# PSUM copies moved to ScalarE and spread over all banks outside the attention loops of a four-layer transformer kernel

## The chip, the cores and the metric

The kernel runs on one core of one Trainium2 chip. The metric is the device time of one launch in microseconds. TensorE (PE) multiplies matrices and transposes, VectorE (DVE), ScalarE (ACT) and GpSimd (POOL) work on elements, SyncE (SP) issues the DMAs.

## The reference

The input is one sequence of 2048 tokens of 512 bf16 features. Four residual layers A, B, A, B are applied, each to a layernorm of its input; both A layers share their weights, and so do both B layers.

```
A: q = x@wq (32 heads of 16); k = x@wk, v = x@wv (one head of 16, shared by all)
   o = softmax(q k^T / 4) v ;                       x += concat(o) @ wo
B: q,k,v = x@wqkv (32 heads of 16); phi(t) = where(t>0, t+1, exp(t)) + 1e-6
   o = phi(q) (phi(k)^T v) / (phi(q) . sum phi(k) + 1e-6) ;  x += concat(o) @ wo2
```

## The kernel before

Tokens lie in 16 tiles of 128 rows; x stays in SBUF (`x_sb`) from the first load to the last store. PSUM is one tensor of 8 banks (`ps_all`, `bank(i)`).

The order of the work is planned when the program is built. `add(engine, tau, ...)` gives each instruction a planned time tau, and each engine's instructions are issued in the order of tau. The tau only sort: the chip waits on semaphores, and each engine's queue is strictly in order. `plan(tau, task)` defers a part of the planning to its turn. A `Chain` is one PSUM bank with the event that last read it; a new user of the bank waits for that event.

The stages in order of time are:

1. **First prologue** (`a_prologue`). One DMA brings all of x, six more bring the weights, all counted on one semaphore, so that the first user of a weight (`ev_w`) waits for the last of them. Per tile, `ln_tile` computes layernorm (L305 statistics, L306 and L307 small steps on DVE, L309 a power on POOL, L314 the normalised tile into one of two `xn_buf` slots), PE transposes it (L322), DVE copies it to `xnT` (L325); `proj_session` (PE at L336) gives V, copied at L360. After every fourth tile, `block_task` gives four blocks of queries (L373) and the replicated keys (L379). Only banks 6 and 7 (`chain6`, `chain7`) are used, and DVE does every copy out of PSUM.
2. **Attention loop** (`a_loop`): 683 groups, in each three score matmuls into three banks (L449; banks 0 to 2 and 3 to 5 in turn), one exponential over them on ACT (L459) and twelve small matmuls with V (L478). After 8 units of a row tile its epilogue runs in bank 7: transposes (L517), copy (L522), output product (L534), residual add to x (L537). `on_x` then plans layer B's preparation of that tile (`b_prep_tile`): layernorm, key, value and, every fourth tile, four query projections, one after the other through bank 7. `phi_session` is one projection with phi: min(x,0) (L560) and max(x,0)+1e-6 (L561) on DVE, exp on ACT (L565), sum on DVE (L566). For tiles 0 to 14 this lies inside the loop, for tile 15 behind it.
3. **Layer B** (`b_main`): 64 matmuls gather phi(k)^T v (L619), four masked copies (L627), then per tile numerator and denominator (L646), two reciprocals (L661) and two products (L663), transpose (L675), copy (L685, DVE), output product (L693), residual add (L697). It uses banks 0 to 5.
4. The second layer A's prologue is planned tile by tile into the first `b_main`, behind each tile's residual add. Then the second loop and the second `b_main` follow, and 16 DMAs store x.

Of the kernel before, what the change touches and what calls it, by code (L numbers as in the profile page):

```python
# [150 lines left out]
def bass_interleave_layers__grouped_kv_mqa__linear_attn_block__prompt_kernel(  # L151
# [36 lines left out]
    xn_buf = sb("xn_buf", [P, 2, D], BF16)  # L188
# [76 lines left out]
    ev_x.tau = 8.0
    add(SP, 0.01, lambda e: e.dma_start(wk_sb[:], A_wk.rearrange("(ft f) c -> f ft c", f=P)), s_wdma, 16)
    add(SP, 0.02, lambda e: e.dma_start(wv_sb[:], A_wv.rearrange("(ft f) c -> f ft c", f=P)), s_wdma, 16)
    add(SP, 0.03, lambda e: e.dma_start(wq_sb[:], A_wq.rearrange("(ft f) c -> f ft c", f=P)), s_wdma, 16)
# [34 lines left out]
    def ln_tile(t, x_ev, tau, chain):
# [21 lines left out]
        evc = add(DV, evt.tau + 0.7 + HOP, lambda e, t=t, tpv=tpv: e.tensor_copy(xnT[:, :, t * P:(t + 1) * P], tpv), dv_a, waits=[evt])  # L325
# [3 lines left out]
    def proj_session(chain, tau, mml, ncols, w_mm, readers):  # L329
# [10 lines left out]
        for (eng, dtau, fn, sem_, xw) in readers:  # L340
            tr = _tmax(tr + dtau, [evm] + list(xw))
            evr = add(eng, tr, (lambda e, fn=fn, dst=dst: fn(e, dst)), sem_, waits=[evm] + list(xw))
            evs.append(evr)
# [451 lines left out]
```

## Time and profile before

| | us |
|---|---|
| median of 4 runs | 2143.38 (2143.09 to 2143.96) |
| the profiled execution | 2143.65 |
| its span, first to last instruction | 2141.8 |
| ACT busy in the span | 1880.0 (88%) |
| PE busy | 1737.6 (81%) |
| DVE busy | 571.3 (27%) |

The 1.85 us between the span and the time of that execution lie outside its instructions. The share of a busy engine is an average over stages: in the loops ACT is full, outside them it is nearly idle.

### The profile page before, as it was taken

The page shows a single profiled execution, that of the slowest core. Times are in us where ns is not written, and L with a number is a line of the kernel's source. Part 1 is how long each engine was busy: PE and PEld are TensorE (multiplying, and loading weights), DVE is VectorE, ACT ScalarE, POOL GpSimd, SP SyncE. Part 2 cuts the span into 40 slices and gives each one's busy share as a digit, 9 for nine tenths or more (in the row PEclk, how much of TensorE's full clock was granted, in tenths as well). Part 3 has the DMA queues.
Part 4 walks back from the last instruction along what each step waited for, and adds up shares of the span by engine and source line. Part 5 has one row for each costly group of instructions (what it writes and reads, how often), then busy time and mean ns, then how long its engine had stood idle before and what let it go on. Part 6 is the DMA issues. An engine that isn't in the chain of part 4 may idle for free.

```text
span 2141.8 us, 49091 instructions
## 1 busy us (share of the span) xinstructions
PE 1737.6 (81%) x22176; PEld 1011.1 (47%) x22176; DVE 571.3 (27%) x1648; ACT 1880.0 (88%) x1431; POOL 42.1 (2%) x80
## 2 busy tenths in 40 slices
PE   4888888888888888887678888888888888888876
PEld 2454454545455454444234544544544454444533
DVE  5221222112322222111680222322213121321227
ACT  0799999999999999998009999999999999999960
POOL 2000000000000000000010000000000000000000
PEclk9999999999999999999799999999999999999988
DMA  3000000000000000000000000000000000000001
GB/s 99 1 1 2 2 2 2 2 2 1 2 2 2 2 2 2 1 2 2 1 1 2 2 1 2 2 2 1 2 2 1 2 2 2 1 2 2 1 1 40
DMA packets 7746, 10.52 MB, mean 5 GB/s; under 512 B 1392, under 2 KB 7024, under 8 KB 7536
## 3 DMA queue, kind: packets, MB, share of 16 engines
q1 hardware_dynamic: 7536, 7.37, 1.1%
q8 instruction: 174, 2.85, 0.6%
q14 instruction: 36, 0.29, 0.0%
HBM read 5.28 MB, written 2.10 MB: 3 GB/s over the span
## 4 chain that ended last, share of the span: by engine, by line
ACT 43%; PE 36%; issue 11%; DVE 9%; DMA 0%; SPq 0%; POOL 0%; ACTq 0%; POOLq 0%
ACT PT L459 42%; PE ps_all L449 20%; PE ps_all L478 8%; PE ps_all L336 5%; PE ps_all L534 1%; ACT e_buf L565 1%; DVE Osb L663 1%; DVE Osb L501 1%; DVE x_sb L697 1%; DVE rdenA L495 1%; DVE stats L305 1%; DVE QT_sb L373 1%; PE ps_all L619 1%; DVE rdenB L661 1%; DVE xnT L325 0%
## 5 line engine op out<-in xcount | busy, mean ns | idle before, releaser
L459 ACT ACTIVATE PT<-ps_all 128x1536 bf16<-128x1536 f32 (+1 forms) x1366 | 1851.6, 1492 | 165.3 <-PE ps_all L449 163.4
L449 PE MATMUL ps_all<-qbd,Krep_sb 128*128 128x512 bf16 x4096 | 1115.1, 381 | 215.2 <-ACT PT L459 215.0
L478 PEld LDWEIGHTS ps_all<-Vaug,PT 128*128 128x128 bf16 x16384 | 619.4, 96 | 433.3 <-DVE Osb L501 110.8
L478 PE MATMUL ps_all<-Vaug,PT 128*128 128x17 bf16 x16384 | 640.2, 171 | 92.9 <-DVE Osb L501 91.1
L449 PEld LDWEIGHTS ps_all<-qbd,Krep_sb 128*128 128x128 bf16 x4096 | 301.0, 97 | 488.6 <-ACT PT L459 269.0
L495 DVE RECIPROCAL rdenA<-ps_all 128x4 f32<-128x4 f32 x256 | 46.7, 182 | 1152.2 <-PE ps_all L478 1152.2
L432 DVE TENSOR_TENSOR qbd<-QT_sb,mask 128x512 bf16<-128x512 bf16 x256 | 102.3, 416 | 0.0
L565 ACT ACTIVATE e_buf<-m_buf 128x512 f32<-128x512 f32 x64 | 41.3, 645 | 47.3 <-DVE m_buf L560 47.3
L309 POOL TENSOR_TENSOR rstd<-veps,mhalf 128x1 f32<-128x1 f32 x64 | 35.1, 548 | 2024.1 <-DVE veps L307 2014.5
L336 PE MATMUL ps_all<-wqkv_sb,xnT 128*128 128x512 bf16 x256 | 69.0, 393 | 3.8 <-DVE r_buf L561 2.8
L560 DVE TENSOR_SCALAR m_buf<-ps_all 128x512 f32<-128x512 f32 x64 | 44.2, 690 | 82.4 <-PE ps_all L336 82.4
L501 DVE TENSOR_TENSOR Osb<-ps_all,rdenA 128x64 bf16<-128x64 f32 x256 | 57.4, 224 | 8.9
L566 DVE TENSOR_TENSOR pk_tok<-e_buf,r_buf 128x512 bf16<-128x512 f32 x32 | 22.1, 692 | 104.2 <-ACT e_buf L565 104.2
L336 PE MATMUL ps_all<-xnT,wqkv_sb 128*128 128x512 bf16 x128 | 39.8, 441 | 11.0 <-DVE r_buf L561 9.2
L305 DVE BATCH_NORM_STATS2 stats<-x_sb 128x6 f32<-128x512 bf16 x64 | 44.1, 689 | 10.9 <-DMA x_sb<-in_A_x_dram 9.8
L336 PE MATMUL ps_all<-xnT,wq_sb 128*128 128x512 bf16 x128 | 40.9, 463 | 7.2 <-DVE QT_sb L373 3.8
L322 PE MATMUL ps_all<-ident,xn_buf 128*128 128x128 bf16 x256 | 27.2, 234 | 22.4 <-DVE xn_buf L314 19.4
L561 DVE TENSOR_SCALAR r_buf<-ps_all 128x512 f32<-128x512 f32 x64 | 43.6, 680 | 0.0
L693 PE MATMUL ps_all<-wo_sb,OT_sb 128*128 128x512 bf16 x128 | 33.1, 381 | 9.2 <-DVE OT_sb L685 9.2
L534 PE MATMUL ps_all<-wo_sb,OT_sb 128*128 128x512 bf16 x128 | 34.2, 390 | 1.0 <-DVE OT_sb L522 1.0
L537 DVE TENSOR_TENSOR x_sb<-x_sb,ps_all 128x512 bf16<-128x512 bf16 x32 | 22.0, 688 | 47.0 <-PE ps_all L534 47.0
L325 DVE COPY xnT<-ps_all 128x512 bf16<-128x512 bf16 x64 | 26.1, 408 | 24.3 <-PE ps_all L322 24.3
(46 smaller groups left out, 415.9 us busy)
## 6 DMA issues: line engine op xcount, KB each, us to landing
x_sb<-in_A_x_dram SPq DMA_DIRECT2D x1, 2048.0 KB, 8.9
out_dram<-x_sb SPq DMA_DIRECT2D x16, 128.0 KB, 1.7
wqkv_sb<-in_B_wqkv_dram SPq DMA_DIRECT2D x1, 1536.0 KB, 8.9
wq_sb<-in_A_wq_dram SPq DMA_DIRECT2D x1, 512.0 KB, 6.4
wo_sb<-in_A_wo_dram SPq DMA_DIRECT2D x1, 512.0 KB, 6.4
wo_sb<-in_B_wo_dram SPq DMA_DIRECT2D x1, 512.0 KB, 9.2
wk_sb<-in_A_wk_dram SPq DMA_DIRECT2D x1, 16.0 KB, 8.4
wv_sb<-in_A_wv_dram SPq DMA_DIRECT2D x1, 16.0 KB, 6.5
```

Source lines behind the costliest of these rows:

```text
L305: ev1 = add(DV, tau, lambda e, t=t: e.bn_stats(stats[:, t, 0:6], x_sb[:, t, :]), dv_a, waits=[x_ev])
L336: evm = add(PE, tp + k * EPS, (lambda e, l=l, r=r, k=k, n=n, dst=dst: e.matmul(dst, lhsT=l, rhs=r, start=(k == 0), stop=(k == n - 1))), pe ...
L432: qbd_ready[u] = add(DV, tq, (lambda e, u=u, qt=qt, g=g, half=half: e.tensor_tensor(out=qbd[:, u % NQBD, :].rearrange("p (a b) -> p a b", ...
L449: ev = add(PE, tsi, (lambda e, dst=dst, t=t, u=u: e.matmul(dst, lhsT=Krep_sb[:, t * P:(t + 1) * P], rhs=qbd[:, u % NQBD, :], start=True, s ...
L459: e_done[j] = add(AC, _tmax(tau_E(j), w), (lambda e, j=j, ng=ng, b0=b0: e.activation(PT[:, j % NPT, 0:ng * 512], bank(b0, ng * 512), ACTF. ...
L478: ev = add(PE, tpv, (lambda e, col0=col0, j=j, idx=idx, hh=hh, t=t: e.matmul(ps_all[:, col0:col0 + 17], lhsT=PT[:, j % NPT, idx * 512 + hh ...
L495: evr = add(DV, tn, (lambda e, accv=accv: e.reciprocal(rdenA[:, :].unsqueeze(2), accv[:, :, DH:DH + 1])), dv_a, waits=[ev_acc])
L501: acc_free[u] = add(DV, _tmax(tn + EPS / 4, wn, d=EPS / 8), (lambda e, qt=qt, quad=quad, accv=accv: e.tensor_tensor(out=Osb[:, qt % 2, qua ...
L534: evy = add(PE, t2 + g * EPS, (lambda e, g=g, qt=qt: e.matmul(bank(7), lhsT=OT_sb[:, qt % 2, g, :], rhs=wo_sb[:, g, :], start=(g == 0), st ...
L560: (DV, 0.0, (lambda e, src, s=s: e.tensor_scalar(out=m_buf[:, s, :], in0=src, scalar1=0.0, scalar2=None, op0=ALU.min)), dv_a, w_m),
L561: (DV, D_EVQ, (lambda e, src, s=s: e.tensor_scalar(out=r_buf[:, s, :], in0=src, scalar1=0.0, scalar2=1e-6, op0=ALU.max, op1=ALU.add)), dv_ ...
L565: ev_e = add(AC, _tmax(ev_m.tau + act_slack, w_e), (lambda e, s=s: e.activation(e_buf[:, s, :], m_buf[:, s, :], ACTF.Exp)), ac_a, waits=w_e)
```

## The change

1. x arrives in four DMAs of four tiles. The first is issued first, then wk, wv and wq on a semaphore of their own (`ev_wA`), then the rest of x and the other weights.
2. Each bank has a chain. `pick_chain` takes the one whose last planned use is oldest, among those that the loops or `b_main` don't hold at that planned time; in both it leaves what it left before (7 in the loop, 6 and 7 in `b_main`).
3. `copy_op` puts a copy on ACT when its planned time lies outside the loops (`act_free`), else on DVE. This holds for `xnT`, V, queries, keys, layer B's values and `OT_sb` of `b_main`.
4. Outside the loops phi's positive part is a Relu on ACT, then the min on DVE, the exp on ACT, and one DVE instruction adds e + 1e-6 + r.
5. Tile 15's preparation for layer B is planned with its six projections side by side in six banks (`parallel=True`). The gathering matmuls of `b_main` no longer wait for phi(q); each fourth tile of `b_main` waits for its block's phi(q).
6. Twelve matmuls whose result is read by nobody (`warm`) stand around the last epilogue of each loop: 2 ahead of the transposes, 2 behind them, 8 behind the output product.
7. `xn_buf` has three slots. Prologue tiles are planned 1.35 apart (1.7 before), block sessions 1.05 (0.6 before).

```diff
+    def act_free(tau):
+        return not _in(act_busy, tau, 2.0, 0.0)
+    def bank_ok(b, tau):
+        if b <= 5:
+            return not _in(s_busy, tau, 4.0, 1.0) and not _in(bmain_busy, tau, 1.0, 1.0)
+        if b == 6:
+            return not _in(act_busy, tau, 4.0, 2.0)
+        return True
+    def copy_op(tau, out_ap_fn, waits, prefer_act=True):
+        if prefer_act and act_free(tau):
+            return add(AC, tau, lambda e: out_ap_fn(e, True), ac_a, waits=waits)
+        return add(DV, tau, lambda e: out_ap_fn(e, False), dv_a, waits=waits)
...
-    ev_x = add(SP, 0.0, lambda e: e.dma_start(x_sb[:], xv), s_xdma, 16)
+    for c in range(4):
+        evd = add(SP, 0.001 * c, lambda e, c=c: e.dma_start(x_sb[:, 4 * c:4 * c + 4, :], xv[:, 4 * c:4 * c + 4, :]), s_xdmas[c], 16)
+        evd.tau = 2.5 * (c + 1)
+    add(SP, 0.0002, lambda e: e.dma_start(wk_sb[:], A_wk.rearrange("(ft f) c -> f ft c", f=P)), s_wA, 16)
+    add(SP, 0.0003, lambda e: e.dma_start(wv_sb[:], A_wv.rearrange("(ft f) c -> f ft c", f=P)), s_wA, 16)
+    ev_wA = add(SP, 0.0004, lambda e: e.dma_start(wq_sb[:], A_wq.rearrange("(ft f) c -> f ft c", f=P)), s_wA, 16)
...
+        L_end = tau_E(NGR) + 0.5
+        act_busy.append((L0, L_end))
+        s_busy.append((L0 - 2.5, L_end))
...
+        def warm(tau, n):
+            for k in range(n):
+                add(PE, tau + k * EPS / 8, (lambda e: e.matmul(bank(5), lhsT=Krep_sb[:, 0:P], rhs=QT_sb[:, 0, 0:512], start=True, stop=True)), None)
...
     def phi_session(chain, tau, mml, dst_ap, w_mm, act_slack):
+        if act_free(tau):
+            evs = proj_session(chain, tau, mml, 512, w_mm, [
+                (AC, 0.0, (lambda e, src, s=s: e.activation(r_buf[:, s, :], src, ACTF.Relu)), ac_a, w_m),
+                (DV, 0.6, (lambda e, src, s=s: e.tensor_scalar(out=m_buf[:, s, :], in0=src, scalar1=0.0, scalar2=None, op0=ALU.min)), dv_a, w_m),
+            ], serial=True)
...
+            ev_fin = add(DV, _tmax(ev_e.tau + 0.7 + HOP, [ev_e, ev_r]), (lambda e, s=s, dst_ap=dst_ap: e.scalar_tensor_tensor(
+                out=dst_ap, in0=e_buf[:, s, :], scalar=1e-6, in1=r_buf[:, s, :], op0=ALU.add, op1=ALU.add)), dv_a, waits=[ev_e, ev_r])
...
+            def ptask2():
+                RB["pk"][t] = phi_session(pick_chain(base), base, mml, pk_tok[:, t, :], [ev_xnT, ev_w], act_slack)
+                base += 4 * EPS
+                mml = [(xnT[:, ft, t * P:(t + 1) * P], wqkv_sb[:, ft, 2 * D:3 * D]) for ft in range(FT)]
+                evs = proj_session(pick_chain(base), base, mml, 512, [ev_xnT, ev_w], [
+                    ("copy", 0.0, mk_copy(lambda src, t=t: (vaugB_v[:, t, :, 0:DH], src.rearrange("p (h d) -> p h d", d=DH))), None, [ev_onesB])])
...
+                    for g in range(NG8):
+                        mml = [(wqkv_sb[:, ft, g * P:(g + 1) * P], xnT[:, ft, b * 512:(b + 1) * 512]) for ft in range(FT)]
+                        RB["pq"][(g, b)] = phi_session(pick_chain(base), base, mml, pqT[:, g, b * 512:(b + 1) * 512], xw, act_slack)
+                        base += 4 * EPS
...
-        w_all = list(RB["pk"]) + list(RB["v"]) + list(RB["pq"].values())
+        w_all = list(RB["pk"]) + list(RB["v"]) + [chains[b].last for b in range(6)]
...
-            evc = add(DV, _tmax(evt.tau + 0.7 + HOP, wc), (lambda e, t=t, tpv=tpv: e.tensor_copy(OT_sb[:, t % 2, :, :], tpv)), dv_a, waits=wc)
+            evc = copy_op(_tmax(evt.tau + 0.7 + HOP, wc), (lambda e, is_act, t=t, tpv=tpv: (e.copy if is_act else e.tensor_copy)(OT_sb[:, t % 2, :, :], tpv)), wc)
...
                 def on_x(qt, evx, RB=RB):
+                    if evx.tau > L_end - 12.0:
+                        b_prep_tile(qt, evx, RB, act_slack=0.3, gap=0.2, parallel=True)
+                    elif evx.tau > L_end - 40.0:
+                        b_prep_tile(qt, evx, RB, act_slack=0.3, gap=0.2)
+                    else:
+                        b_prep_tile(qt, evx, RB, act_slack=8.0, gap=1.0)
```

## Rows read from the trace of the kernel before

**Rows 1.** Busy time per engine in the stages, cut at the stage boundaries.
```profile
core 0: us, PE busy (x) PEld busy (x) DVE busy (x) ACT busy (x) POOL busy (x), PEclk, DMA share, GB/s
0.00:69.30 69.30, 38.25 (x213) 17.01 (x214) 39.37 (x118) 1.31 (x2) 15.79 (x32) 0.90 0.24 77
69.30:1012.80 943.50, 788.90 (x10585) 468.73 (x10583) 200.19 (x583) 936.16 (x710) 8.22 (x15) 1.00 0.01 2
1012.80:1048.20 35.40, 19.64 (x100) 8.87 (x100) 14.44 (x29) 3.15 (x5) 0.55 (x1) 0.57 0.00 0
1048.20:1123.60 75.40, 55.30 (x404) 26.45 (x405) 68.65 (x214) 0.00 (x0) 8.77 (x16) 0.98 0.00 1
```

**Rows 2.** Timeline of the first prologue: start us, us, engine, line, operation.
```profile
5.02 1.47 SPq L268 DMA_DIRECT2D wq_sb<-in_A_wq_dram  x1
...
9.77 0.69 DVE L305 BATCH_NORM_STATS2 stats<-x_sb 128x6 f32<-128x512 bf16 x1 [9.77 <-DMA x_sb<-in_A_x_dram]
...
12.74 0.41 DVE L325 COPY xnT<-ps_all 128x512 bf16<-128x512 bf16 x1
...
18.36 0.76 POOL L296 COPY wk_rep<-wk_sb 128x128 bf16<-128x128 bf16 x3 [5.50 <-DMA wo_sb<-in_B_wo_dram]
...
25.39 1.89 PE L336 MATMUL ps_all<-xnT,wq_sb 128*128 128x512 bf16 x4 [0.41 <-DVE Vaug L360]
...
63.04 1.04 PE L336 MATMUL ps_all<-xnT,wk_rep 128*128 128x512 bf16 x4 [0.70 <-DVE QT_sb L373]
...
69.27 8.16 ACT L459 ACTIVATE PT<-ps_all 128x1536 bf16<-128x1536 f32 x6 [67.18 <-PE ps_all L449]
```

**Rows 3.** Groups of ACT by shape: count, busy us, mean ns.
```profile
L459 ACT ACTIVATE PT<-ps_all 128x1536 bf16<-128x1536 f32 x1364 | 1849.7, 1493 | 165.3 <-PE ps_all L449 163.4
L565 ACT ACTIVATE e_buf<-m_buf 128x512 f32<-128x512 f32 x64 | 41.3, 645 | 47.3 <-DVE m_buf L560 47.3
L459 ACT ACTIVATE PT<-ps_all 128x1024 bf16<-128x1024 f32 x2 | 2.1, 1056 | 0.0
L459 ACT ACT_TABLE_LOAD x1 | 1.3, 1283 | 0.8 <-PEq L780 0.8
```

**Rows 4.** Groups of DVE by shape, from 1042 to 1126 us.
```profile
L373 DVE CAST QT_sb<-ps_all 128x512 bf16<-128x512 f32 x16 | 10.9, 680 | 3.0 <-PE ps_all L336 3.0
...
L685 DVE COPY OT_sb<-ps_all 128x512 bf16<-128x512 bf16 x16 | 6.6, 410 | 0.5 <-PE ps_all L675 0.5
...
L325 DVE COPY xnT<-ps_all 128x512 bf16<-128x512 bf16 x16 | 6.0, 378 | 0.2 <-PE ps_all L322 0.2
```

**Rows 5.** Timeline behind the first loop, tile 15's epilogue to `b_main`.
```profile
1016.17 0.69 DVE L537 TENSOR_TENSOR x_sb<-x_sb,ps_all 128x512 bf16<-128x512 bf16 x1 [1.98 <-PE ps_all L534]
...
1020.26 1.89 PE L336 MATMUL ps_all<-wqkv_sb,xnT 128*128 128x512 bf16 x4 [0.52 <-DVE xnT L325]
...
1041.79 5.42 PE L619 MATMUL ps_all<-vaugB,pk_tok 128*128 128x136 bf16 x64 [3.88 <-DVE pqT L566]
```

**Rows 6.** Timeline of the first `b_main` with the second prologue in it.
```profile
1048.22 0.41 PE L646 MATMUL ps_all<-kvzbd,pqT 128*128 128x136 bf16 x4 [1.01 <-DVE kvzbd L627]
...
1058.34 0.68 DVE L697 TENSOR_TENSOR x_sb<-x_sb,ps_all 128x512 bf16<-128x512 bf16 x1
...
1061.72 0.68 DVE L697 TENSOR_TENSOR x_sb<-x_sb,ps_all 128x512 bf16<-128x512 bf16 x1
...
1110.11 0.69 DVE L697 TENSOR_TENSOR x_sb<-x_sb,ps_all 128x512 bf16<-128x512 bf16 x1
...
1116.78 5.29 PE L336 MATMUL ps_all<-xnT,wq_sb 128*128 128x512 bf16 x16 [0.27 <-DVE Vaug L360]
...
1123.62 4.14 ACT L459 ACTIVATE PT<-ps_all 128x1536 bf16<-128x1536 f32 x3 [84.32 <-PE ps_all L449]
```

**Rows 7.** Timeline of the second `b_main`: its second and its fifteenth residual add.
```profile
2108.64 0.68 DVE L697 TENSOR_TENSOR x_sb<-x_sb,ps_all 128x512 bf16<-128x512 bf16 x1
...
2136.89 0.68 DVE L697 TENSOR_TENSOR x_sb<-x_sb,ps_all 128x512 bf16<-128x512 bf16 x1
```

More of the change, by code (lines that the diff above doesn't have):

```diff
@@ L259, in start_tau @@
             return tau
-    chain6 = Chain(6)
-    chain7 = Chain(7)
-    ev_x = add(SP, 0.0, lambda e: e.dma_start(x_sb[:], xv), s_xdma, 16)
[L265 to L268, printed above, removed]
+    chains = [Chain(b) for b in range(8)]
@@ new lines, in pick_chain @@
+    def pick_chain(tau, dur=2.5):
+        best = None
+        for ch in chains:
+            if not (bank_ok(ch.bank, tau) and bank_ok(ch.bank, tau + dur)):
+                continue
+            lt = ch.last.tau if ch.last is not None else -1.0
+            if best is None or lt < best[0]:
+                best = (lt, ch)
+        assert best is not None
+        return best[1]
+    def copy_op(tau, out_ap_fn, waits, prefer_act=True):
+        if prefer_act and act_free(tau):
+            return add(AC, tau, lambda e: out_ap_fn(e, True), ac_a, waits=waits)
+        return add(DV, tau, lambda e: out_ap_fn(e, False), dv_a, waits=waits)
@@ L324, in ln_tile, with cp, proj_session @@
         ln_state["xn_last_reader"][slot] = evt
-        evc = add(DV, evt.tau + 0.7 + HOP, lambda e, t=t, tpv=tpv: e.tensor_copy(xnT[:, :, t * P:(t + 1) * P], tpv), dv_a, waits=[evt])
+        def cp(e, is_act, t=t, tpv=tpv):
+            if is_act:
+                return e.copy(xnT[:, :, t * P:(t + 1) * P], tpv)
+            return e.tensor_copy(xnT[:, :, t * P:(t + 1) * P], tpv)
+        evc = copy_op(evt.tau + 0.7 + HOP, cp, [evt])
         chain.last = evc
         return evc
-    def proj_session(chain, tau, mml, ncols, w_mm, readers):
+    def proj_session(chain, tau, mml, ncols, w_mm, readers, serial=False):
         tp = chain.start_tau(_tmax(tau, list(w_mm)))
@@ L340, in proj_session @@
         for (eng, dtau, fn, sem_, xw) in readers:
-            tr = _tmax(tr + dtau, [evm] + list(xw))
-            evr = add(eng, tr, (lambda e, fn=fn, dst=dst: fn(e, dst)), sem_, waits=[evm] + list(xw))
+            wr = [evm] + list(xw)
+            if serial and evs:
+                wr.append(evs[-1])
+            tr = _tmax(tr + dtau, wr)
+            if eng == "copy":
+                evr = copy_op(tr, (lambda e, is_act, fn=fn, dst=dst: fn(e, dst, is_act)), wr)
+            else:
+                evr = add(eng, tr, (lambda e, fn=fn, dst=dst: fn(e, dst)), sem_, waits=wr)
             evs.append(evr)
@@ L413, in tau_seg @@
             return L0 + (j + 1) * TG + 0.05
+        L_end = tau_E(NGR) + 0.5
+        act_busy.append((L0, L_end))
+        s_busy.append((L0 - 2.5, L_end))
+        st["L_end"] = L_end
+        astate["L_end"] = L_end
+        s_init_wait = [chains[b].last for b in range(6)]
         def group_task(j):
@@ L460, in group_task @@
                 PT[:, j % NPT, 0:ng * 512], bank(b0, ng * 512), ACTF.Exp, scale=SCALE)), ac_e, waits=w)
+            if j >= NGR - NSETS:
+                for bb in range(b0, b0 + G):
+                    chains[bb].last = e_done[j]
             tpv = _tmax(tau_seg(j) + 0.02, [e_done[j]])
@@ L639, in b_main @@
             w = [ev_bd] if t == 0 else []
+            if t % 4 == 0:
+                w += [RB["pq"][(g, t // 4)] for g in range(NG8)]
             if nd_read[s_] is not None:
```

153 lines of the change are left out of this document (113 added, 40 removed).

## The prediction

> **What bounds the kernel now.** I read the busy time by stage first. The two attention loops take 943.5 us each and ACT is busy for 936 of that [rows 1]: there the exponentials set the pace, and the edits leave the loop's instructions on the engines and banks that they had. What can change are the five other stretches: the first prologue (69.3 us), the piece behind each loop up to the per-tile part of layer B (35.4 us, twice), the first `b_main` with the second prologue inside it (75.4 us) and the second `b_main` (39 us, the rest of the span): 255 us in all. In these ACT is almost unused: 0 us of 75.4, 3.15 of 35.4, 1.3 of 69.3 [rows 1]. DVE is busy for 68.65 of the 75.4 us [rows 1], so there the copies out of PSUM are in the way. Behind the loops nothing is busy: PE 19.6 us of 35.4 at a mean granted clock of 0.57 [rows 1]. That is a chain of latencies through one bank, and the timeline shows it: six projections one after the other need 21.5 us, from 1020.26 to 1041.79 [rows 5]. In the first prologue the timeline shows two waits for DMA: the first statistics at 9.77 us, and the first use of a weight at 18.36 us, behind the last of the weights [rows 2].
>
> TensorE's level is read from matmuls: four of 512 columns need 1.89 us at 25.39 [rows 2] and 1020.26 [rows 5], which is the lower of the levels (1.2 GHz), and 1.04 us at 63.04 [rows 2], the upper (2.4 GHz; without the last one's latency some 0.9).
>
> **The price of an ACT copy.** No row shows ACT copying, so I bound it. Exponentials out of PSUM take 1493 ns for 1536 columns and 1056 for 1024 [rows 3], a step of 437 per 512, so 512 columns would be 1056 - 437 = 619 ns; out of SBUF they take 645 [rows 3]. By the same slope 16 columns come to about 0.2 us. In a row they can follow each other faster: 1849.7 us busy for 1364 of 1493 ns [rows 3] is 1.36 each, 0.13 less than the duration. So 0.49 to 0.65; I take 0.62. DVE needs 680 ns for the same from fp32 and 378 to 410 from bf16 [rows 4]. So a moved query copy costs nothing by itself, and a moved `xnT` or `OT_sb` copy adds 0.2 us to its chain, while DVE is relieved. The Trainium skill (ScalarE: Activation LUTs, section "Rules for kernel authors") speaks against the move: it wants relu and the like on VectorE, up to about three times faster in bf16. By that rule a 512-column ACT copy would be near 3 x 0.41 = 1.23 us, an estimate; that is the second rival below. For the fp32 copies, 0.68 us on DVE [rows 4] against the 0.62 worked out for ACT, the rows don't show such a ratio; no run here shows the bf16 one.
>
> Copy and Relu beside Exp may need a table load. The one load in the trace takes 1.283 us [rows 3]. Both ends: nothing, or about 12 switches (one at the end of each prologue, four behind each loop, two more around `b_main`), 15 us. I take nothing and keep the 15 for the range, because no row decides it.
>
> **First prologue: 25 us less.** From 9.77 to 18.36 us the other weights, 3.07 MB, came in behind x: 0.36 MB/us [rows 2]. With 1.5 MB of x out of the way the first quarter is there 4.2 us earlier, at about 5.6. wq is still the fourth DMA in SP's queue, issued from 5.02 for 1.47 us [rows 2], so `ev_wA` can't come before 6.5; I take 8. The three later quarters of x are behind it in the queue, but 1.5 MB at that rate is in by 13, before its tiles are due. POOL's replication of wk now waits at its early place in POOL's queue, and the powers of tiles 2 and 3 wait behind it, until 8: small. Tile 0's `xnT` came 3.0 us after its statistics (12.74 against 9.77), and from the weights to the first query block it was 7.0 us (18.36 to 25.39) [rows 2]. Put together: 5.6 + 3.4 + about 6 = 15. From there PE has 20 projections of four matmuls at 0.95 and 12 tiles' transposes and V at some 0.55: 25.6 us, plus 2.5 because it starts at the lower level for 5 us or so, plus 1.2 for the last copy and the first scores: the first exponential at 44 instead of 69.27 [rows 2]. ACT alone has 36 x 0.62 + 16 x 0.2 = 25.5 us of copies in the stage, so it runs level with PE and is not ahead; DVE has far less. Bounds: 37 if the steps overlap well and the upper level comes at once; 62 if PE stays at the lower level (20 x 1.85 + 12 x 0.85 = 47 after 15). Gain 25, from 7 to 32.
>
> **Behind each loop: 14 us less, twice.** With six banks the projections run back to back: two at 1.85 and the rest at 0.95. ACT's queue is strict, and by the planned times the Exp of the key stands behind four Relus and a copy, so it waits for the fifth projection: 2 x 1.85 + 3 x 0.95 = 6.6, then Relu 0.62, Exp 0.62, the sum on DVE 0.69: 8.5 us instead of 21.5. phi(q), which `b_main` no longer waits for, runs on DVE and ACT under the 64 gathering matmuls (5.42 us [rows 5]); if it were late, the first tile waits, some 2 us. The gathering itself starts at the upper level, 0.8 less. The twelve warm matmuls lie in PE's gaps: the 8, at most 8 x 0.47 = 3.8 us, under the layernorm of tile 15, which has 1020.26 - 1016.86 = 3.4 us behind the residual add [rows 5]; without that cover they'd cost 0.4. So 13 + 0.8. Bounds: 16.5 with the upper level throughout, 10.5 with the lower. Twice: 28, from 21 to 33.
>
> **First `b_main` and second prologue: 15 us less.** Of DVE, the copies of `OT_sb`, `xnT`, queries, keys and V go to ACT. A tile without projections takes 1061.72 - 1058.34 = 3.38 us [rows 6], with DVE the busy engine; without its two copies (0.41 and 0.38 long, about 0.5 of them not overlapped) and V's, 2.8. With projections PE sets it: 55.3 us busy [rows 1], less 5 for the last block, over 16 tiles is 3.15; I take 3.2. ACT's share per tile, three copies and V's, is 2.2: covered. So the last residual add comes 4 + 5 x 2.8 + 10 x 3.2 = 50 us after the stage's begin (before: 1110.11 - 1048.22 = 62 [rows 6]). Behind it come the last layernorm, 3.4 us, and five projections that began at the lower level (16 matmuls in 5.29 us [rows 6]), and the first exponential: 10 us (before 13.5). 60 instead of 75.4. Bounds: not below PE's 52 or so, 23 less; at worst 6 less, if PE waits for ACT's longer copy in every tile.
>
> **Second `b_main`: 1 us less.** Its period is (2136.89 - 2108.64) / 13 = 2.17 us [rows 7]. The copy leaves DVE, but it sits 0.2 us longer between transpose and output product, and the residual add waits for that product: about 2.1. 15 x 0.07 = 1, from 3 less to 2 more.
>
> The sum: 25 + 28 + 15 + 1 = 69, against the profiled 2143.65 (the median is 0.27 lower, less than this sum can tell): about 2074 us.
>
> **The rivals.**
> *PE stays at the lower level.* Copies on ACT put a 0.62 us wait behind every transpose, and behind the loop the level fell although PE was busy for more than half of the time [rows 1]. Then 7 + 21 + 6 - 1 = 33 less: 2111. Against it: denser matmuls, and the level rose within the 16 matmuls at 1116.78 [rows 6]. 13 in 100. The Trainium skill (TensorE: Matmul & The Clock Gate, section "Part 4: PE-mode transpose") says that transposes do not count as busy in the same way, which speaks for this rival in the prologues, where every tile has four of them; no row of this trace shows transposes alone.
> *ACT becomes the bound.* If an ACT copy took three times DVE's 0.41 [rows 4], 1.23 us, the first prologue's ACT work doubles: 36 x 1.23 + 3 = 47 after 9, gain 13; the stage with the second prologue needs 16 x 4.2 = 67 and gains about 3; behind the loops 11 twice. 38 less: 2106. The rows on ACT speak against it. 6 in 100.
> *Slower: copies inside the loops.* If the planner's spans miss and Relus and copies of layer B's preparation go onto ACT in the loop, the 57 instructions of a loop (15 tiles with two copies and one Relu, 12 query Relus) hit the engine that is full. At 0.62 plus half of 1.04 us of waiting for the projection they cost 114 x 1.14 = 130 us: 2205. From 111 such instructions without any wait the 69 are gone. Against it: the planned time of these operations lies within (L0, L_end). 3 in 100.
> *Nothing changes outside the first DMAs* (planned times of tile 15 inside the span): about 2143. 1 in 100.
> *Better overlap.* Upper level early, ACT copies at 0.49: up to 32 + 33 + 23 = 88 less, about 2055 or a bit below. 15 in 100.
>
> **How the numbers follow.** My forecast, 2060 to 2095, has 62 in 100. The range of 8 in 10 reaches from 2052 to 2103: it takes in the better overlap in part, the 15 us of table loads, and half of the way to the cold rival. What this kernel's measurement can tell from no change is 0.2%, some 4.3 us. Faster 0.95, same 0.01, slower 0.04.
>
> **What the profile will show.** Right: a first exponential near 44 us; gathering matmuls some 9 us behind tile 15's `xnT`; ACT busy in the stages outside the loops; the stage from the first numerator to the first exponential of the second loop near 60 us; loops of 943 us. Wrong: loops longer than 944 us, 512-column ACT copies near 1.2 us, more than one table load, or four matmuls at 1.89 us through the prologues.

## The result and the profile after

The changed kernel takes 2070.53 us (median of 8 runs, 2068.09 to 2070.83) against 2143.46 (13 runs): a ratio of 0.9658, with a 95% interval of 0.9648 to 0.9667. That is 3.5 us below the predicted 2074.0 and inside both ranges of the forecast. The profiled execution took 2070.58 us with a span of 2068.9.

Busy time by stage of the changed kernel, cut as in [rows 1], with the second piece behind the loop and the second `b_main` as well:

```profile
core 0: us, PE busy (x) PEld busy (x) DVE busy (x) ACT busy (x) POOL busy (x), PEclk, DMA share, GB/s
0.00:41.10 41.10, 28.70 (x212) 13.84 (x213) 20.60 (x67) 22.81 (x54) 15.72 (x32) 1.00 0.40 129
41.10:984.60 943.50, 788.78 (x10586) 468.72 (x10585) 199.57 (x580) 936.18 (x710) 8.21 (x15) 1.00 0.01 2
984.60:1002.70 18.10, 13.76 (x113) 7.70 (x110) 10.34 (x22) 6.75 (x12) 0.55 (x1) 1.00 0.01 2
1002.70:1067.10 64.40, 52.39 (x405) 27.60 (x406) 49.31 (x147) 31.47 (x69) 8.76 (x16) 0.95 0.00 1
...
2010.60:2028.70 18.10, 14.97 (x113) 8.24 (x110) 9.43 (x18) 6.75 (x12) 0.55 (x1) 0.91 0.00 1
2028.70:2068.90 40.20, 27.75 (x196) 12.93 (x193) 31.07 (x84) 9.36 (x16) 0.00 (x0) 0.96 0.16 53
```

The loops kept their 943.5 us and ACT's 936 in them. Everything gained lies outside. In the table the stages are cut at single instructions (the first exponential, the last normalisation of the loop, the first numerator), so that they add up to the span.

| us | before | after | gain | predicted gain |
|---|---|---|---|---|
| to the first exponential | 69.27 | 41.09 | 28.2 | 25 |
| first and second loop | 943.78, 943.77 | 943.77, 943.78 | 0 | 0 |
| behind the loops, to the first numerator | 35.17, 35.21 | 17.85, 19.06 | 17.3 and 16.2 | 14 and 14 |
| first `b_main` with second prologue | 75.40 | 64.37 | 11.0 | 15 |
| second `b_main` to the end | 39.23 | 38.93 | 0.3 | 1 |
| span | 2141.83 | 2068.86 | 73.0 | 69 |

**The copies on ACT.** Groups of ACT by shape, as in [rows 3]:

```profile
L372 ACT COPY xnT<-ps_all 128x512 bf16<-128x512 bf16 x34 | 20.2, 593 | 27.6 <-PE ps_all L367 27.4
L823 ACT COPY OT_sb<-ps_all 128x512 bf16<-128x512 bf16 x32 | 18.8, 587 | 41.7 <-PE ps_all L813 41.6
L406 ACT CAST QT_sb<-ps_all 128x512 bf16<-128x512 f32 x32 | 18.8, 589 | 7.0 <-PE ps_all L385 6.9
L648 ACT ACTIVATE r_buf<-ps_all 128x512 f32<-128x512 f32 x10 | 5.9, 594 | 3.9 <-PE ps_all L385 3.9
L372 ACT ACT_TABLE_LOAD x1 | 1.3, 1283 | 0.8 <-PEq L932 0.8
```

Copy, cast and Relu all cost 0.59 us, and one table load is all there is.

**First prologue.** Its timeline, to be read beside [rows 2]:

```profile
2.37 0.51 SPq L311 DMA_DIRECT2D wq_sb<-in_A_wq_dram  x1
...
5.05 0.70 DVE L349 BATCH_NORM_STATS2 stats<-x_sb 128x6 f32<-128x512 bf16 x1 [5.05 <-DMA x_sb<-in_A_x_dram]
...
9.01 0.28 PE L385 MATMUL ps_all<-wv_sb,xnT 128*128 128x16 bf16 x4 [0.68 <-ACT xnT L372]
...
13.24 0.59 PE L385 MATMUL ps_all<-xnT,wq_sb 128*128 128x512 bf16 x1
...
15.41 1.91 PE L385 MATMUL ps_all<-xnT,wq_sb 128*128 128x512 bf16 x4
...
17.65 1.03 PE L385 MATMUL ps_all<-xnT,wq_sb 128*128 128x512 bf16 x4
...
41.09 4.13 ACT L530 ACTIVATE PT<-ps_all 128x1536 bf16<-128x1536 f32 x3 [0.48 <-PE ps_all L520]
```

The statistics now wait for the first quarter of x alone, and V no longer waits for the last weight but for its own copy. Four query matmuls fall from 1.91 to 1.03 us at 17.65, so the upper level (2.4 GHz) is there 4.4 us after the first query matmul.

**Behind the first loop**, beside [rows 5]:

```profile
987.13 0.69 DVE L623 TENSOR_TENSOR x_sb<-x_sb,ps_all 128x512 bf16<-128x512 bf16 x1 [1.13 <-PE ps_all L618]
...
991.16 1.90 PE L385 MATMUL ps_all<-wqkv_sb,xnT 128*128 128x512 bf16 x8 [0.68 <-ACT xnT L372]
...
992.90 3.62 PE L385 MATMUL ps_all<-xnT,wqkv_sb 128*128 128x512 bf16 x16
...
996.18 2.18 ACT L653 ACTIVATE e_buf<-m_buf 128x512 f32<-128x512 f32 x4
...
997.00 0.68 DVE L654 SCALAR_TENSOR_TENSOR pk_tok<-e_buf,r_buf 128x512 bf16<-128x512 f32 x1
...
997.74 3.96 PE L755 MATMUL ps_all<-vaugB,pk_tok 128*128 128x136 bf16 x64 [1.22 <-DVE pk_tok L654]
...
1002.71 0.41 PE L784 MATMUL ps_all<-kvzbd,pqT 128*128 128x136 bf16 x4 [1.01 <-DVE kvzbd L763]
```

All six projections run as two groups, eight matmuls in 1.90 us: the upper level from the first on. The gathering matmuls start 6.58 us behind the first projection (21.53 before), and the numerator waits for `kvzbd`, not for phi(q).

**First `b_main`**, beside [rows 6]: four of its 16 residual adds, and two windows, the first over five tiles without block projections, the second over the nine tiles in which the block projections lie:

```profile
1007.77 0.69 DVE L835 TENSOR_TENSOR x_sb<-x_sb,ps_all 128x512 bf16<-128x512 bf16 x1 [0.77 <-PE ps_all L831]
1010.76 0.69 DVE L835 TENSOR_TENSOR x_sb<-x_sb,ps_all 128x512 bf16<-128x512 bf16 x1
...
1025.57 0.68 DVE L835 TENSOR_TENSOR x_sb<-x_sb,ps_all 128x512 bf16<-128x512 bf16 x1
...
1056.18 0.69 DVE L835 TENSOR_TENSOR x_sb<-x_sb,ps_all 128x512 bf16<-128x512 bf16 x1 [1.37 <-PE ps_all L831]
```

```profile
1010.76:1025.57 14.81, 10.46 (x100) 6.07 (x101) 14.46 (x45) 6.54 (x14) 2.74 (x5) 0.99 0.00 0
1025.57:1056.18 30.61, 27.19 (x223) 14.66 (x221) 26.19 (x78) 17.56 (x39) 4.93 (x9) 1.00 0.00 1
```

A tile without projections takes 14.81/5 = 2.96 us, and DVE is still busy for 14.46 of the 14.81. With them it is 30.61/9 = 3.40 on the mean (from 2.97 to 3.67), with PE busy for 27.19 of 30.61.

### The profile page after: what moved, and what is told of

Its sections match the earlier page's. It is cut to its first block, busy times and chain, and to the rows that moved or that the text cites. A ratio compares the mean times of both kernels' runs of the same rounds, so it can differ in the third digit from the quotient of the medians.

```text
span 2068.9 us, 49164 instructions
## 1 busy us (share of the span) xinstructions
PE 1715.2 (83%) x22200; PEld 1007.8 (49%) x22200; DVE 519.9 (25%) x1498; ACT 1949.5 (94%) x1581; POOL 42.0 (2%) x80
## 4 chain that ended last, share of the span: by engine, by line
ACT 46%; PE 38%; issue 12%; DVE 3%; POOL 0%; ACTq 0%; POOLq 0%; DVEq 0%
ACT PT L530 43%; PE ps_all L520 21%; PE ps_all L552 8%; PE ps_all L385 4%; PE ps_all L831 1%; PE ps_all L618 1%; ACT e_buf L663 1%; DVE Osb L575 1%; DVE rdenA L569 1%; PE ps_all L367 1%; ACT OT_sb L823 1%; ACT xnT L372 0%; PE ps_all L813 0%; PE ps_all L755 0%; PE ps_all L599 0%
## 5 line engine op out<-in xcount | busy, mean ns | idle before, releaser
L823 ACT COPY OT_sb<-ps_all 128x512 bf16<-128x512 bf16 x32 | 18.8, 587 | 41.7 <-PE ps_all L813 41.6
L658 DVE TENSOR_SCALAR m_buf<-ps_all 128x512 f32<-128x512 f32 x54 | 37.3, 690 | 63.7 <-PE ps_all L385 63.7
L372 ACT COPY xnT<-ps_all 128x512 bf16<-128x512 bf16 x34 | 20.2, 593 | 27.6 <-PE ps_all L367 27.4
L659 DVE TENSOR_SCALAR r_buf<-ps_all 128x512 f32<-128x512 f32 x54 | 36.8, 681 | 0.0
L663 ACT ACTIVATE e_buf<-m_buf 128x512 f32<-128x512 f32 x54 | 35.0, 648 | 0.0
L385 PE MATMUL ps_all<-xnT,wq_sb 128*128 128x512 bf16 x128 | 33.7, 394 | 1.1 <-ACT Krep_sb L406 1.0
L618 PE MATMUL ps_all<-wo_sb,OT_sb 128*128 128x512 bf16 x128 | 33.6, 385 | 0.1
```

What stands on the lines that cost most here:

```text
L385: evm = add(PE, tp + k * EPS, (lambda e, l=l, r=r, k=k, n=n, dst=dst: e.matmul(dst, lhsT=l, rhs=r, start=(k == 0), stop=(k == n - 1))), pe ...
L618: evy = add(PE, t2 + g * EPS, (lambda e, g=g, qt=qt: e.matmul(bank(7), lhsT=OT_sb[:, qt % 2, g, :], rhs=wo_sb[:, g, :], start=(g == 0), st ...
L663: ev_e = add(AC, _tmax(ev_m.tau + act_slack, w_e), (lambda e, s=s: e.activation(e_buf[:, s, :], m_buf[:, s, :], ACTF.Exp)), ac_a, waits=w_e)
```

## The experiments

Each stands on its own change from the changed kernel, except "DMA order alone", which starts from the kernel before. Ratios are to the kernel before, run on the same chip. Stage times are of the profiled execution, in the order of the table above:

| kernel | median us | ratio (95%) | prologue | behind loops | first `b_main` | second | span |
|---|---|---|---|---|---|---|---|
| the change | 2070.53 | 0.9658 (0.9648 to 0.9667) | 41.09 | 17.85, 19.06 | 64.37 | 38.93 | 2068.9 |
| the change, again | 2069.36 | 0.9656 (0.9642 to 0.9669) | 41.09 | 17.85, 18.71 | 63.08 | 39.01 | 2067.3 |
| DMA order alone | 2134.75 | 0.9958 (0.9943 to 0.9973) | 60.44 | 35.15, 35.21 | 75.40 | 39.32 | 2133.1 |
| copies on DVE | 2093.47 | 0.9768 (0.9754 to 0.9783) | 48.86 | 20.39, 20.42 | 73.52 | 39.26 | 2090.0 |
| two banks | 2085.85 | 0.9732 (0.9718 to 0.9747) | 54.97 | 19.34, 18.18 | 64.84 | 39.92 | 2084.8 |
| no warm matmuls | 2074.69 | 0.9682 (0.9666 to 0.9698) | 40.83 | 20.92, 20.87 | 63.08 | 37.88 | 2071.1 |
| `OT_sb` on DVE | 2075.44 | 0.9685 (0.9668 to 0.9701) | 41.08 | 17.85, 17.85 | 66.49 | 39.27 | 2070.1 |
| xn on ACT | 2076.39 | 0.9687 (0.9673 to 0.9702) | 41.73 | 19.00, 17.85 | 70.33 | 39.01 | 2075.5 |
| key first | 2076.57 | 0.9688 (0.9673 to 0.9702) | 41.60 | 22.22, 22.33 | 64.39 | 38.95 | 2077.1 |
| warm in `b_main` | 2067.13 | 0.9645 (0.9631 to 0.9659) | 41.07 | 17.85, 17.86 | 63.10 | 37.88 | 2065.4 |
| warm in `b_main`, again | 2067.53 | 0.9648 (0.9634 to 0.9661) | 41.32 | 17.85, 17.86 | 63.08 | 37.88 | 2065.5 |
| best | 2066.74 | 0.9646 (0.9633 to 0.9659) | 41.09 | 16.97, 16.97 | 64.61 | 37.87 | 2065.1 |

**1. DMA order alone.** The kernel before with only the four DMAs of x, the early weights and their own semaphore.

```diff
...
-    t_ = 12.5
+    t_ = 6.5
...
-    x_evs = [ev_x] * T
-    tau = 9.0
+    x_evs = list(x_dma_evs)
+    tau = 3.0
```

The four DMAs themselves and the semaphore `ev_wA` are the lines of the change, shown above.

> The kernel before with nothing but the new order of the DMAs, the two semaphores and the earlier planned times that go with it. Theory: the first V product starts some 9.5 us earlier (18.4 us before, 9.0 in the changed kernel), everything behind it moves with it, and the first exponential comes at about 60 us instead of 69.3: 2134 us, a third of the first prologue's 28 us. Rival: VectorE is the bound from the first statistics on, so that only their 4.7 us (9.77 to 5.05) come through: 2138.5 us.

Measured: 8.8 us less in the first prologue, nothing elsewhere, as expected. From the timeline of the prologue:

```profile
16.04 1.89 PE L342 MATMUL ps_all<-xnT,wq_sb 128*128 128x512 bf16 x4 [0.41 <-DVE Vaug L366]
```

The first query matmul comes 9.35 us sooner than in [rows 2], and 44.4 us of prologue remain behind it (27.85 in the changed kernel). So of the 28.2 us gained here the DMAs alone give a third.

**2. Copies on DVE.** No copy and no Relu goes to ACT; banks, DMAs, order and warm matmuls stay.

```diff
     def act_free(tau):
-        return not _in(act_busy, tau, 2.0, 0.0)
+        return False
```

> The changed kernel with every copy out of PSUM, and phi's positive part, on VectorE again; banks, order, DMAs and warm matmuls stay. Theory: banks alone give back part, and VectorE becomes the bound where it was: the first exponential at about 47 us (41.1 in the changed kernel), the stage from the first numerator to the second loop's first exponential at 75 (64.4, before 75.4), behind each loop 20 (18 to 19): 2090 us. Rival: the banks are all that matters and the engine of the copies is worth nothing, 2071 to 2075; or the engine is all that matters, 2125 or more.

Measured: 21.1 us more span (22.9 between the medians). Of them 9.2 are in the first `b_main`, 7.8 in the first prologue, 2.5 and 1.4 behind the loops; the expectation came close in each stage. The window over the first `b_main` shows DVE full again, 69.5 of 73 us, as in [rows 1]:

```profile
1013.00:1086.00 73.00, 53.36 (x394) 26.00 (x403) 69.50 (x215) 0.00 (x0) 8.80 (x16) 1.00 0.00 1
```

**3. Two banks.** Outside the loops only banks 6 and 7 are open to `pick_chain`; tile 15's projections share them too.

```diff
         if b <= 5:
-            return not _in(s_busy, tau, 4.0, 1.0) and not _in(bmain_busy, tau, 1.0, 1.0)
+            return False
```

> The changed kernel with copies on ScalarE, but only banks 6 and 7 for the prologues and for tile 15's six projections. Theory: the stage with the second prologue has these two banks anyway and stays at 64.4 us; the first prologue loses 2 to 4 us; behind each loop a projection holds its bank for 0.9 + 0.6 + 0.7 us, so six of them in two banks take 2 us more each time: 2078 us. Rival: the banks carry most of the gain and the time goes back beyond 2100 us.

Measured: 13.9 us more in the first prologue, several times what I expected there, and 2.0 in all elsewhere, less than expected. The planner sets its times by the banks, so the order of the work changes with them, and the run gives the price of both together. PE's timeline and one wait of DVE:

```profile
25.94 0.38 PE L367 MATMUL ps_all<-ident,xn_buf 128*128 128x128 bf16 x4 [0.97 <-ACT xnT L372]
...
27.25 0.38 PE L367 MATMUL ps_all<-ident,xn_buf 128*128 128x128 bf16 x4 [0.84 <-ACT xnT L372]
...
33.21 1.49 PE L385 MATMUL ps_all<-xnT,wq_sb 128*128 128x512 bf16 x3 [1.15 <-ACT xnT L372]
```

```profile
25.09 0.41 DVE L359 TENSOR_SCALAR xn_buf<-x_sb,mv,rstd 128x512 bf16<-128x512 bf16 x1 [5.81 <-PE ps_all L367]
```

With two banks a block's five projections go as one piece between tiles, and DVE waits 5.81 us for a free `xn_buf`; then tiles follow in lockstep, transposes, copy, V, 1.31 us each, with PE idle for most of it, and at 33.21 three query matmuls take 1.49 us: the level has fallen. The banks let projections of one block fill the gaps of the next block's tiles. Behind the loops the times are 1.5 us longer and 0.9 shorter: there two banks in turn are nearly as good as six.

**4. No warm matmuls.** The twelve whose result nobody reads are left out.

```diff
-            for k in range(n):
+            for k in range(0):
```

> The changed kernel without its twelve warm matmuls behind each loop. Theory: they are what keeps TensorE at its upper level there. The output product of tile 15 then takes 1.89 us instead of 1.04 and the first two projections 1.85 instead of 0.95 each, so each of the two pieces behind the loops grows from 18.1 and 19.3 us to about 20.5: 2074 us. Rival (what the prediction said of them): they only fill gaps and do nothing, 2070.5 us.

Measured: 3.1 and 1.8 us more behind the loops; 2.2 us more span, 4.2 between the medians. PE's timeline behind the first loop:

```profile
991.72 3.60 PE L385 MATMUL ps_all<-wqkv_sb,xnT 128*128 128x512 bf16 x8 [0.68 <-ACT xnT L372]
```

Eight projection matmuls take 3.60 us instead of 1.90: the lower level, behind a layernorm under which PE had nothing to do. Behind them the first `b_main` is 1.3 us and the second 1.1 us shorter than in the profiled execution of the change, since the upper level holds there. That this comes from leaving the twelve out is not shown: the change again had the same 63.08 in the first, and number 9, which has the twelve, had 37.88 in the second. Two of the four executions of this kernel took 3.4 us longer than the profiled one (2076.3 and 2076.4 against 2072.9), and their stages are not known.

**5. Warm matmuls at the start of `b_main`.** Four more behind the gathering matmuls, while DVE masks, and six behind the first numerator, all into bank 5.

```diff
+        def junk(tau, n):
+            for k in range(n):
+                add(PE, tau + k * EPS / 16, (lambda e: e.matmul(bank(5), lhsT=Krep_sb[:, 0:P], rhs=QT_sb[:, 0, 0:512], start=True, stop=True)), None)
+        junk(ev_kvz.tau + EPS / 4, 4)
...
+            if t == 0:
+                junk(evnd.tau + EPS / 4, 6)
```

> The changed kernel with ten more warm matmuls at the begin of each layer B: four behind the gathering matmuls and six behind the first tile's numerator. Theory: the 1.0 us and 1.4 us in which TensorE stands still there let its level fall, so that in the changed kernel the first transposes take 0.61 us and the first two output products 1.89 instead of 1.04; kept up, the first residual add comes 1.2 us earlier in each layer B: 2068 us. Rival: the fall has another cause, or the ten matmuls delay the numerators as much as they help, 2070.5 us or more.

It was run once more beside the change itself:

> The kernel with ten more warm matmuls once more, to measure it beside the changed kernel on one chip. Theory: 2067 us, 3 us below the changed kernel. Rival: the difference seen was between chips or executions, and both agree within 1 us.

> The changed kernel itself beside the two others. Theory: 2070.5 us as before. Rival: none; it is the base of the comparison.

Measured: 2067.13 and 2067.53 against 2070.53 and 2069.36. Side by side, in the second runs of both, that is 1.8 us: between the 3 that I expected and the 1 of the rival, and the intervals of the two ratios overlap. The windows over the first tiles of `b_main`: the change, the change again, and this kernel (second run).

```profile
1002.70:1010.00 7.30, 5.41 (x27) 2.84 (x28) 4.71 (x15) 1.17 (x2) 0.33 (x1) 0.59 0.01 2
```

```profile
1002.70:1010.00 7.30, 4.09 (x35) 2.15 (x36) 5.74 (x17) 1.17 (x2) 0.55 (x1) 1.00 0.01 2
```

```profile
1002.90:1010.00 7.10, 5.15 (x37) 2.42 (x38) 5.50 (x17) 1.17 (x2) 0.55 (x1) 1.00 0.01 2
```

The same kernel had a granted clock of 0.59 there in one execution and of 1.00 in another, and the first residual add came 5.06 or 4.00 us after the numerator; the stage took 64.37 or 63.08. With the ten matmuls it was 1.00 in both profiled executions, and the second `b_main` took 37.9 us, not 39.0. Over the first tiles of either `b_main` the granted clock fell at three of four such places in the two profiled executions of the change, and at none of six in those of numbers 5 and 10, which have the ten. It can hold without them too, as number 4 shows.

**6. `OT_sb` on DVE.** Only the copy of `b_main` goes back.

```diff
-            evc = copy_op(_tmax(evt.tau + 0.7 + HOP, wc), (lambda e, is_act, t=t, tpv=tpv: ...), wc)
+            evc = copy_op(_tmax(evt.tau + 0.7 + HOP, wc), (lambda e, is_act, t=t, tpv=tpv: ...), wc, prefer_act=False)
```

> The changed kernel with only the transposed output's copy in layer B back on VectorE. Theory: VectorE is the busy engine in the first layer B; 0.33 us more per tile there give 5 us back (64.4 to 69), and the second layer B's period goes from 2.08 to 2.17 us, 1 us back: 2076.5 us. Rival: ScalarE's longer copy (0.59 against 0.41 us) between transpose and output product is what holds the period, and the stage gets shorter, 2067 us.

Measured: the first `b_main` 2.1 us longer than the profiled change, 3.4 longer than the change again; less than I had set for it. The profiled execution was the shortest of the four (2071.88; the median is 2075.44), so what the others lost besides is not seen. Tiles without projections take 3.16 us (adds at 1010.57, 1013.73, 1016.88) instead of 2.96, so of 0.41 us of copy given back to DVE half shows. The copy is back between the statistics (1014.65) and their aggregate (1015.57):

```profile
1015.25 0.41 DVE L823 COPY OT_sb<-ps_all 128x512 bf16<-128x512 bf16 x1
```

**7. xn on ACT.** If DVE sets the tile, taking more off it should help: in the second prologue the normalised tile is made on ACT, with a small step on POOL ahead.

```diff
...
+            ev4b = add(PO, ..., lambda e, t=t: e.tensor_scalar(out=nmr[:, t:t + 1], in0=mv[:, t, 0:1], scalar1=rstd[:, t:t + 1], scalar2=-1.0, op0=ALU.mult, op1=ALU.mult), ...)
...
+            ev5 = add(AC, tx, lambda e, t=t, slot=slot: e.activation(xn_buf[:, slot, :], x_sb[:, t, :], ACTF.Identity, bias=nmr[:, t:t + 1], scale=rstd[:, t:t + 1]), ac_a, waits=[ev4b, wr])
```

> The changed kernel with the normalised tile of the second prologue written by ScalarE (rstd * x - mean * rstd, the product by GpSimd) instead of VectorE. Theory: in tiles without projections VectorE sets the period of 2.96 us; without 0.33 us of it per tile, and with the projections' tiles less bound by it, the stage from the first numerator goes from 64.4 to about 60: 2066 us. Rival: TensorE's order and the waits through ScalarE set the 3.4 us of the tiles with projections, and ScalarE's and GpSimd's extra steps delay the transposes: no gain, 2070 us or more.

Measured: the stage grew from 64.37 to 70.33 us. From the timeline, a tile without projections and a tile with them:

```profile
1021.93 0.82 ACT L364 ACTIVATE xn_buf<-x_sb,nmr,rstd 128x512 bf16<-128x512 bf16 x1
...
1023.35 1.04 PE L839 MATMUL ps_all<-wo_sb,OT_sb 128*128 128x512 bf16 x4 [0.75 <-ACT OT_sb L831]
...
1030.10 2.01 PE L393 MATMUL ps_all<-xnT,wq_sb 128*128 128x512 bf16 x8
...
1033.01 0.69 DVE L843 TENSOR_TENSOR x_sb<-x_sb,ps_all 128x512 bf16<-128x512 bf16 x1 [1.55 <-PE ps_all L839]
```

After two tiles of 2.77 us a tile without projections takes up to 3.20 us (adds at 1021.23 and 1024.42) instead of 2.96: the 0.82 us of xn stands ahead of the copy of `OT_sb` in ACT's queue, and the output product waits 0.75 us for that copy. But most of the 6 us lies in three tiles, one with each later block of projections, which take 5.4 us where the change has 3.4 to 3.6. There the residual add waits 1.55 us for an output product that PE runs only behind eight query matmuls. My expectation fell: with xn off DVE it is the order of the steps between the engines that sets the tile. Which of the moved steps brings the query matmuls ahead is not shown.

**8. Key first.** The query projections are planned 0.9 us apart, so that the key's Exp goes out ahead of their Relus.

```diff
-                        base += 4 * EPS
+                        base += 0.9
```

> The changed kernel with the four query projections of tile 15 planned 0.9 apart, so that ScalarE's queue holds the Exp of the key ahead of the later Relus. Theory: the key's sum is then ready before the last projection, and the gathering matmuls wait only for TensorE: they start 1.2 us earlier behind each loop, 2068 us. Rival: the piece is bound by TensorE or by VectorE's queue and stays, 2070.5 us.

Measured: 4.4 and 3.3 us more behind the loops in the profiled execution, the longest of the four; my expectation fell. The sum of the key and the gathering matmuls:

```profile
998.89 0.68 DVE L654 SCALAR_TENSOR_TENSOR pk_tok<-e_buf,r_buf 128x512 bf16<-128x512 f32 x1
...
1001.06 3.16 PE L755 MATMUL ps_all<-vaugB,pk_tok 128*128 128x136 bf16 x34 [2.88 <-DVE m_buf L649]
```

The key's sum is at 998.89, yet the matmuls wait 2.88 us for a min of the queries: `w_all` holds the last readers of six banks, though the matmuls write two. So they start 2.8 of the 4.4 us later; the other 1.6 lie between them and the numerator, 6.59 us apart instead of 4.97, at a granted clock of 0.74 instead of 1.00. In the change phi(q) is not out of the way either; it is hidden only while its readers of the banks are early.

**9. Copies in the loops too.** What the slower rival feared: 57 instructions of each loop go to ACT.

```diff
     def act_free(tau):
-        return not _in(act_busy, tau, 2.0, 0.0)
+        return True
```

> The changed kernel with its copies and phi's Relu on ScalarE inside the attention loops too (the prediction's slower rival made real). Theory: ScalarE is full there; 57 instructions of 0.59 us per loop (15 tiles with two copies and a Relu, 12 query Relus) cost at least 34 us per loop and with the waits for their projections up to 65: 2140 to 2200 us. Rival: the loop hides them, for instance in ScalarE's waits for the scores, and the time stays below 2100 us.

Measured, one execution: 2134.75 us, span 2132.7, 63.8 more than the change. ACT's groups in the first loop:

```profile
L648 ACT ACTIVATE r_buf<-ps_all 128x512 f32<-128x512 f32 x27 | 16.7, 618 | 4.7 <-PE ps_all L385 4.7
L406 ACT CAST vaugB<-ps_all 128x512 bf16<-128x512 f32 x15 | 9.7, 645 | 0.0
L372 ACT COPY xnT<-ps_all 128x512 bf16<-128x512 bf16 x15 | 8.8, 586 | 6.4 <-PE ps_all L367 5.9
```

The loops grew by 33.6 and 32.8 us, and the stretches outside them were 2.5 us shorter than in the profiled change. 66.4/114 = 0.58 us each, half of the 1.14 that I had worked out in the prediction. They cost their own length (35.2 us of ACT in the first loop); the waits of the copies there (6.4 and 4.7 us) don't come on top. The time lies just below the 2140 that I had set as the lower end, and far above the rival's 2100.

**10. Best.** Number 5, with the key's Exp early, and the wait of the gathering matmuls cut to the two banks that they write; the first numerator waits for the others. For the first, the key's planned delays are made smaller as well.

```diff
-        w_all = list(RB["pk"]) + list(RB["v"]) + [chains[b].last for b in range(6)]
+        w_all = list(RB["pk"]) + list(RB["v"]) + [chains[b].last for b in range(2)]
+        w_nd1 = [chains[b].last for b in range(2, 6) if chains[b].last is not None]
...
+            if t == 0:
+                w += w_nd1
...
-                        base += 4 * EPS
+                        base += 0.7 if g == 0 else 0.15
```

> The changed kernel with the ten more warm matmuls at the begin of layer B; the Exp of tile 15's key ahead of the last two query Relus and its sum ahead of their mins; and the gathering matmuls waiting only for the readers of banks 0 and 1, which they write, while the first numerator waits for the others. Theory: the planned order of the key's Exp lost in the earlier trial because the gathering matmuls waited for the mins of banks that they don't write; with that wait gone they start when TensorE is free, about 1 us earlier per loop: 2065 us. Rival: VectorE's order still holds them, 2067 us or more.

Measured: 16.97 us behind both loops, 0.88 less than in number 5, since the gathering matmuls start at 996.70, not at 997.74 as in the change, whose first exponential is at the same 41.09:

```profile
996.70 3.95 PE L756 MATMUL ps_all<-vaugB,pk_tok 128*128 128x136 bf16 x64 [0.19 <-DVE m_buf L649]
```

But the first `b_main` took 1.5 us longer than in number 5, with a granted clock of 0.82 over its last projections (1057.0 to 1066.4). At 2066.74 us it lies below the change; from number 5 (2067.13, 2067.53) it can't be told apart.

## Why the prediction was right

**The price of a copy held.** 0.587 to 0.594 us for 512 columns against 0.62, inside 0.49 to 0.65; 0.17 for V against 0.2. One table load, so the 15 us kept for the range fall away; the Trainium skill (ScalarE: Activation LUTs, section "Table sets: the hidden batching unit") says that copy, identity and relu are filler in every set, and the trace agrees. The factor of up to three in bf16 that the Trainium skill (ScalarE: Activation LUTs, section "Rules for kernel authors") gives VectorE for relu and the like isn't reached by these copies out of PSUM: 0.59 us against DVE's 0.41, 1.4 times, and from fp32 ACT is the faster, 0.59 against 0.68 [rows 4].

**First prologue: 28.2 for 25, inside 7 to 32.** By steps: statistics 4.7 us sooner (4.2 predicted), from there to the first query matmul 7.4 less (6.2, from 15.62 to 9.4), from that matmul to the first exponential 16.0 less (14.9). V ran at 9.01, as the sum had it (5.6 + 3.4), and the weights were there by then: POOL's copy of wk, which waits for all three, starts at 8.31. The term that was too large is the next one, "about 6" from V to the first query matmul: it took 4.2 us (9.01 to 13.24), the V products of the four tiles following each other every 1.4 us. The cause was three things at once, as the text had them: without the ACT copies 7.8 us of the gain are lost, without the banks 13.9, and DMAs alone give 8.8. The first two are taken away from the changed kernel and the third is put onto the kernel before, so they don't add up, and what the DMAs are worth on top of the rest no run shows; nor does any the third slot of `xn_buf` or the new planned distances alone. The banks were given no price of their own in the prediction, though they cost more to lose here than the engine of the copies.

**Behind the loops: 17.3 and 16.2 for 14.** The bounds were 10.5 and 16.5, so the first lies 0.8 above them. By marks it is: last normalisation to residual add 0.85 us less (0 predicted), residual add to first projection 0.06, from there to the gathering matmuls 14.95 (13), and from these to the numerator 1.46 (0.8). The mis-sized term is the level: I let the first two projections run at 1.85 us each and the warm matmuls only fill gaps; number 4 shows that they keep the upper level through the projections, 1.90 us for two. The order was as predicted: the key's Exp stands behind four Relus and a copy, and the gathering starts when the key's sum ends (997.00 + 0.68).

The prediction put the gain down to six banks, and that did not come out. With two banks the pieces were 1.5 us longer and 0.9 shorter, with the copies on DVE 2.5 and 1.4 longer, without the warm matmuls 3.1 and 1.8 longer: together less than half of 17.3 and 16.2. What is left is the planning side by side and the dropped wait for phi(q). In the kernel before, a projection waited for the last reader of the one before it:

```profile
1029.47 1.89 PE L336 MATMUL ps_all<-xnT,wqkv_sb 128*128 128x512 bf16 x4 [1.38 <-DVE r_buf L561]
```

In the changed kernel the last phi(q) is ready at 1001.47 (1000.78 + 0.69), 3.7 us behind the start of the gathering. Had the old wait stood and all else been the same, the gathering would have started there: an estimate of 3.7 of the 14.95 us for the dropped wait, and the rest for the planning with the level. No run takes the two apart.

**First `b_main`: 11.0 for 15, inside 6 to 23.** Last residual add 53.5 us after the first numerator (50 predicted), the rest 10.9 (10). Tiles took 2.96 and 3.40 us where I had 2.8 and 3.2, and the first one 5.06 for 4. DVE stayed the busy engine in the tiles without projections, and their 3.38 us became 2.96: 0.42 less, where I had counted 0.58. DVE's rows say where the rest is, before and after:

```profile
1062.73 0.68 DVE L305 BATCH_NORM_STATS2 stats<-x_sb 128x6 f32<-128x512 bf16 x1
1063.33 0.41 DVE L685 COPY OT_sb<-ps_all 128x512 bf16<-128x512 bf16 x1
1063.65 0.17 DVE L306 BATCH_NORM_AGGREGATE mv<-stats 128x2 f32<-128x6 f32 x1
```

```profile
1014.65 0.69 DVE L349 BATCH_NORM_STATS2 stats<-x_sb 128x6 f32<-128x512 bf16 x1
1015.37 0.18 DVE L350 BATCH_NORM_AGGREGATE mv<-stats 128x2 f32<-128x6 f32 x1
```

From one start to the next the three copies had taken 0.32 (`OT_sb`), 0.28 (`xnT`) and 0.09 us (V) of DVE's queue, 0.69 in all. But the copy of `OT_sb` lay between the statistics and the aggregate that reads them: with it the aggregate started 0.92 us behind the statistics, without it still 0.72, so only 0.20 is won. The copy of `xnT` lay in the same way between a reciprocal and its product, 0.44 us apart with it and 0.28 without. Number 6 puts one copy back and loses just the 0.20. A copy that fills a gap between two dependent steps is worth less to move than its length. The first tile's 1.06 us is the level, which came and went between executions (number 5).

**Second `b_main`: 0.3 for 1.** The period fell to 27.01/13 = 2.08 us (adds at 2036.96 and 2063.97), from 2.17 and as predicted; but the second residual add came 7.04 us after the numerator (6.04 before), with a granted clock of 0.76 until then. Where the level held (numbers 4, 5, 9 and 10) the gain is 1.35.

**The rivals.** The lower level didn't stay: four matmuls at 1.03 us from 17.65 on. ACT as the bound is out at 0.59 us. The table of stages refutes "nothing outside the DMAs", and number 1 gives its price: 8.8. The slower rival's place was right and its price was not: 0.58 us for an instruction in the loop, not 1.14, so all 114 of them cost 66, and the kernel is still 9 us faster than before; "111 such instructions" would not have undone the change. In the sum errors of both signs met: the prologue and the pieces behind the loops gave 8.6 more than predicted, both `b_main` 4.7 less. That the total came within 4 us of 69 is in part luck.

## What to carry to other kernels

Where one engine is full in the loops and empty around them, price the stages around them one by one; copies out of PSUM can change engine there as long as the planned times keep them out of the loop. Count banks and clock level as terms of their own: here the banks beyond the first two were worth more in the first prologue than the engine of the copies (13.9 and 7.8 us), and a dozen unread matmuls around a layernorm 2 to 4 us. Before counting a copy's length as gain, look at what stands next to it: of the 0.69 us that three copies took of DVE's queue per tile, 0.27 had filled waits between other steps. Before more work is moved, look at the queue into which it goes: number 7 took work off the busiest engine and lost 6 us, since copies and products that others waited for came later.

## What the runs showed of the hardware that was not expected

The level of TensorE at one place is not the same in all executions of one kernel (0.59 and 1.00 at the start of `b_main`, number 5). The Trainium skill (TensorE: Matmul & The Clock Gate, section "What's actually happening") says so of the start of a kernel, "it's run-variable"; here it is seen 1000 us later. What decides between the two stays open.

The column of the granted clock can be wrong at the start: for the first 41.1 us of the changed kernel it shows 1.00, while four matmuls at 15.41 take 1.91 us. The trace holds no record of the clock before 17.64 us, and ahead of that the level is read from matmuls alone.

The same DMA of wq took SP 1.47 us to issue behind all of x [rows 2] and 0.51 behind a quarter of it. What sets this time is not shown.
